# Retention, routed experts and a gated layer on one core: when weight conversions, piece remainders and routing steps are issued

## The chip, the cores and the metric

One core of a Trainium2 chip runs the whole program in one launch. The metric is the time of one launch in device microseconds (us); the profile's own span runs from the first to the last instruction of one profiled launch. TensorE (PE) multiplies, VectorE (DVE) and ScalarE (ACT) work on SBUF and PSUM, GpSimd (POOL) works on SBUF and issues the indirect DMAs, and the sync engine (SP) issues all other DMAs.

## The reference, cut to what matters

Three stages follow one another. Retention over 768 steps gives 3072 tokens of 512 numbers. The router gives each token to one of eight experts with room for 384 tokens each, in the order of the sorted logits; each expert is two matrix products with a relu. A gated layer then works on every token.

```python
# routed experts
order = np.argsort(-flat)                       # flat = (x @ w_gate).flatten()
for idx in order:                               # greedy, cap = N // E = 384
    tok, e = idx // E, idx % E
    if assigned[tok] >= 0 or counts[e] >= cap: continue
    assigned[tok] = e; counts[e] += 1
for e in range(E):
    out[mask] = np.maximum(x[mask] @ w1[e], 0.0) @ w2[e]
# gated layer
gate = 1.0 / (1.0 + np.exp(-(x @ w_gate)))
return gate * (x @ w_val) @ w_out
```

## The kernel before, in words

**Stages.** Retention runs first, 24 blocks of 128 tokens (lines 453 to 492), with 23 of 36 weight conversions woven in. The first routing phase follows alone (lines 822 to 823), then eight experts, each with its own 384 tokens: the expert's two products (h_step and y_step for eight column blocks f) and, for the same tokens, the gated layer (g_step and o_step for twelve column blocks g). While one expert is computed the routing of the next is found.

**Units.** One unit is twelve products of 128 x 384 (an h_step, a y_step, or the gate or value half of a g_step) or nine products of 128 x 512 (an o_step). After each unit hook() is called (lines 809 to 820): it runs the next piece of the next expert's routing if its delay has run out, and then whatever `late` holds for that unit number. An expert has 51 units, numbered from 0 in the first expert. PE, DVE, ACT and POOL each work in the order in which instructions are issued, so the place of a hook call in the code is its place in every queue.

**Routing.** members(x) (line 553) is a generator whose yields are delays in units. For the first expert it runs at once, on DVE with idle products that keep PE busy; for the later ones search4 (line 308) finds the cut in eight digits. Each digit has two halves: compare (cm, line 291), then, some units later, count on PE (line 299) with own, sm, ex on DVE (lines 301 to 304), then a small product on PE (line 318) with top, fl, ed, edb on DVE (lines 321 to 326) and the next compare. After the eighth digit come the positions, the comparison of line 643, the count of line 646 and the gather of the expert's tokens by three indirect DMAs on POOL (lines 532 to 535). turn_x transposes the gathered tokens in three turns; in the first expert the first turn comes at g == 8, in others at g == 7 (line 862).

**Pieces.** All products read weights split into a rounded part hi (ACT, line 664) and a remainder lo (DVE, line 665), made in a ring of six pieces in a fixed order (lines 679 to 723); ahead(key) makes pieces up to five beyond the one in use.

**Conversions.** The gated layer's weights come as 8-byte numbers; conv_steps (line 147) turns 512 columns into a float block of `wall`: ACT and DVE (lines 153, 154), DVE (156), ACT and POOL (158, 159), DVE (161). A conversion's last 13 of 36 run in the first expert, at units 7, 9, 12, ... by LATE: lines 154 and 156 at unit u, 158 and 159 at u + 1, 161 at u + 3.

Of the kernel before, what the change touches and what calls it, by code (L numbers as in the profile page):

```python
# [20 lines left out]
def retention_moe_glu_kernel(  # L21
# [285 lines left out]

    def search4(x):

        for n in range(8):  # L310
            cm = compare4()
            if n < 7:
                digit4(n + 1)
            yield 2
            ex = count4(cm)
            yield 2 if x == 1 else 1
            pd = psm.tile([128, 128], F32, name="pr")
            PE.matmul(pd, ones16, ex.rearrange("p t e -> p (t e)"), start=True, stop=True)
            if n < 7:
                top, fl, d = small("top", (128, 16)), small("fl4", (128, 16)), small("d", (128, 1))  # L320
                DVE.tensor_reduce(top, pd.rearrange("p (t e) -> p t e", e=E), AX, OP.max)
                DVE.tensor_scalar(fl, top, CAP - 0.5, None, op0=OP.is_gt, op1=OP.add, accum_out=d)
                ed = small("ed")
                DVE.scalar_tensor_tensor(ed, r["edb"], d, far_up, op0=OP.subtract, op1=OP.mult)
                r["edb"] = small("edb", dt=BF)
                DVE.scalar_tensor_tensor(r["edb"], r["d4"][:, n + 1, :], 1.0, ed, op0=OP.add, op1=OP.add)
            else:
                fl, f = small("fle", (128, 16, E)), small("f", (128, E))
                DVE.tensor_scalar(fl, pd.rearrange("p (t e) -> p t e", e=E), CAP - 0.5, None, op0=OP.is_gt)
                DVE.tensor_reduce(f, fl.rearrange("p t e -> p e t"), AX, OP.add)  # L330
                r["full"] = f
# [105 lines left out]

    EARLY = 23
    LATE = [7 + 5 * n // 2 for n in range(NP - EARLY)]
    RAWS = 3  # L440
    conv_at = {4 + n * 41 // EARLY: n for n in range(EARLY)}

# [60 lines left out]

    idxs, xT, W, XG = {}, {}, {}, {}
    def gather(dst, src, col):
        POOL.indirect_dma_start(out=dst, out_offset=None, in_=src,
                                in_offset=bass.IndirectOffsetOnAxis(ap=col, axis=0))
# [32 lines left out]
    def fetch_rest():  # L540

        rest = W[0][0][:, :, 512:]
        ACT.activation(rest[:, 0, :1], ident[:, :1], AF.Copy)
        src = w1[bass.ds(which[0], 1)].rearrange("o (a p) f -> p (o a) f", p=128)
        SP.dma_start(rest, src[:, :, 512:])
        for f in range(2, W2R):
            fetch_w2(0, f)
        for n in range(RAWS):
            conv_load(EARLY + n, main, RAWS)

    which = {}

    def members(x, begun=None):
# [10 lines left out]
        if x < E - 1:  # L564
# [7 lines left out]
            for n in range(NL if x == 0 else 0):  # L572
# [6 lines left out]
                if n + 1 < NL:  # L579
                    digit(n + 1)  # L580
                yield 3 if T > 64 else 2
                pr = psm.tile([128, 128], F32, name="pr")
# [20 lines left out]
            else:  # L603
                yield from search4(x)
                full = r["full"]
# [37 lines left out]
        cms = [compare(i, c0, c1, 128, smb, OP.is_equal) for i, (c0, c1) in enumerate(parts)]  # L643
        yield 3 if x == 1 else 4
        ps = psm.tile([128, 128], F32, name="pr")
# [7 lines left out]
        if x + 1 < E:  # L653
# [5 lines left out]
            DVE.tensor_scalar(r["pen"], w8, mx, -3.0e38, op0=OP.is_equal, op1=OP.mult)  # L659
            DVE.scalar_tensor_tensor(arow, arow, mx, arow, op0=OP.not_equal, op1=OP.mult)  # L660
        yield 1

# [35 lines left out]
    def make(n):  # L698
        while made[0] < min(n, len(order)):
# [11 lines left out]
            t = main.tile([128, 2, DT, 128], F32R, name="piece", bufs=RING)  # L711
            split(src, t[:, 0], t[:, 1], DVE)
            pieces[key] = t
# [18 lines left out]
    def h_step(x, f):  # L732
        w = use(("w1", x, f))
        p = psm.tile([128, CAP], F32, name="mm", bufs=3)
        for dt in range(DT):
            three(p, w, (xT[x][:, 0, dt, :], xT[x][:, 1, dt, :]), dt, dt == 0, dt == DT - 1)
        t = main.tile([128, 2, CAP], F32R, name="hT", bufs=2)
        ACT.activation(t[:, 0], p, AF.Relu)  # L738
# [4 lines left out]
    def y_step(x, f):  # L743
# [3 lines left out]
        for dt in range(DT):  # L747
            three(acc[0][dt], w, (hT[f][:, 0], hT[f][:, 1]), dt, f == 0, f == FB - 1)
        if f == FB - 1:
            t = main.tile([128, 2, DT, CAP], F32R, name="x2T")  # L750
            x2[0] = t
            for dt in range(DT):
                split(acc[0][dt], t[:, 0, dt, :], t[:, 1, dt, :])
        ahead(("w2", x, f))

    def g_step(x, g):
        t = x2[0]
        ps = []
        for kind in ("wg", "wv"):
            w = use((kind, x, g))  # L760
            p = psm.tile([128, CAP], F32, name="mm", bufs=3)
            for dt in range(DT):
                three(p, w, (t[:, 0, dt, :], t[:, 1, dt, :]), dt, dt == 0, dt == DT - 1)
            ps.append(p)
            hook()
            if kind == "wg":
                sg = main.tile([128, CAP], F32, name="sg", bufs=2)
                ACT.activation(sg, p, AF.Sigmoid)
        gv = main.tile([128, CAP], F32, name="gv", bufs=2)
        DVE.tensor_tensor(gv, ps[1], sg, OP.mult)  # L770
        gt = main.tile([128, 2, CAP], F32R, name="gT", bufs=2)
        split(gv, gt[:, 0], gt[:, 1])
        gT[g] = gt
        ahead(("wv", x, g))

    scat = []
    spacer = consts.tile([1, 1], F32, name="spacer")

    def o_step(x, g):
        w = use(("wo", x, g)).rearrange("p z a b -> p z (a b)")  # L780
        if g == 0:
            acc[1] = [psm.tile([128, M], F32, name="acc", bufs=4) for _ in range(NA)]
        for a in range(NA):
            r = slice(a * 128, (a + 1) * 128)
            p = acc[1][a]
            PE.matmul(p, gT[g][:, 0, r], w[:, 0], start=(g == 0), stop=False)  # L786
            PE.matmul(p, gT[g][:, 0, r], w[:, 1], start=False, stop=False)  # L787
            PE.matmul(p, gT[g][:, 1, r], w[:, 0], start=False, stop=(g == GB - 1))  # L788
        if g == GB - 1:
            for a in range(NA):  # L790
                o = main.tile([128, M], F32, name="o", bufs=3)
                if a % 2:
                    DVE.tensor_copy(o, acc[1][a])
                else:
                    ACT.activation(o, acc[1][a], AF.Copy)
                POOL.memset(spacer, 0.0)
                st = POOL.indirect_dma_start(
                    out=out, out_offset=bass.IndirectOffsetOnAxis(ap=idxs[x][:, a:a + 1], axis=0),
                    in_=o, in_offset=None)
                for s in scat:  # L800
                    tc.declare_no_dep(st.ins, s.ins, reason="rows of other tokens")
                scat.append(st)
        ahead(("wo", x, g))
# [28 lines left out]

    late = {}
    for n, u in enumerate(LATE):
        m = EARLY + n
        if n + RAWS < len(LATE):
# [5 lines left out]
    for x in range(E):  # L842
# [4 lines left out]
        for f in range(FB):  # L847
            if f + 1 < FB:
                h_step(x, f + 1)
                hook()  # L850
            y_step(x, f)
            hook()
        g_step(x, 0)
        turn = None
        for g in range(GB):
            if g + 1 < GB:
                g_step(x, g + 1)
            elif x + 1 < E:
                for _ in turn:
                    pass  # L860
                h_step(x + 1, 0)
            if g == (7 if x else 8) and x + 1 < E:
                assert job[0] is None
                turn = turn_x(x + 1)
            if turn is not None:
                next(turn, None)
            o_step(x, g)
            hook()

# [41 lines left out]
```

## Time and profile before

| what | us |
|---|---|
| median of three timed launches (lowest, highest) | 1124.16 (1123.57, 1124.96) |
| the profiled launch, its own time | 1123.29 |
| its span, first to last instruction | 1121.5 |
| retention | 0 to about 152 |
| first routing phase | about 152 to 184 |
| first expert, first product to the next expert's first product | 184.07 to 314.11 |
| a later expert | 115.3 |
| last expert's part with no routing left, and the stores | 1007 to 1121.5 |

In the page each engine has a busy share; in tables by window each row is one stretch with the busy time of each engine and the granted clock of PE; in a timeline each row is start, length, engine, line, operation, output and input, and in brackets the idle time before it with what ended it.

### The profile page before, as it was taken

Reading aid. Unit: us, or ns where it says so; the run is one execution under the profiler, and the core shown is the slowest. Engines: PE = TensorE matmul, PEld = TensorE weight load, DVE = VectorE, ACT = ScalarE, POOL = GpSimd, SP = SyncE. Lnnn points to the kernel's source line nnn. Section 1 sums busy time; section 2 is a strip of 40 time slices with the busy share of each in tenths; the row PEclk is TensorE's granted clock in tenths of the full one; section 3 lists DMA queues with packets and bytes.
Section 4 is the critical chain, followed back from the end, with each engine's and each line's share of the span. In section 5 each row is a group of like instructions: output and inputs, shape, how many; then the busy total and the mean of one; then the engine's idle time right before and its main releaser. Section 6 shows DMA issues by size and latency. Waiting matters only on the chain.

```text
span 1121.5 us, 18122 instructions
## 1 busy us (share of the span) xinstructions
PE 1088.5 (97%) x6964; PEld 1005.2 (90%) x6964; DVE 736.8 (66%) x1787; ACT 487.6 (43%) x955; POOL 134.9 (12%) x146
## 2 busy tenths in 40 slices
PE   8999999988799999999999999999999999999997
PEld 6988988977799999989998999999989999999996
DVE  4887876888667756775677666765676545554542
ACT  3666623554343444334434343344343434343442
POOL 4354401121110011001100110011001000100001
PEclk9999989999899999999999999999999999999999
DMA  9999916123320212012100310031103012101000
GB/s 218 282 261 292 247 39 217 57 75 87 120 76 1 101 31 75 1 57 76 66 11 10 122 57 20 1 132 47 30 1 132 17 60 79 54 23 54 1 1 29
DMA packets 109608, 91.42 MB, mean 82 GB/s; under 512 B 54737, under 2 KB 92625, under 8 KB 109521
## 3 DMA queue, kind: packets, MB, share of 16 engines
q1 hardware_dynamic: 105680, 77.67, 23.4%
q0 software_dynamic: 3840, 12.59, 3.4%
q8 instruction: 55, 0.90, 0.3%
q14 instruction: 33, 0.26, 0.1%
HBM read 77.66 MB, written 12.58 MB: 80 GB/s over the span
## 4 chain that ended last, share of the span: by engine, by line
PE 73%; issue 11%; DVE 11%; SPq 2%; ACT 1%; DMA 1%; POOL 1%; POOLq 0%; DVEq 0%; ACTq 0%
PE mm L726 13%; PE mm L728 12%; PE mm L727 12%; PE acc L786 5%; PE acc L788 5%; PE acc L787 5%; DVE piece L665 3%; PE acc L726 2%; PE acc L728 2%; PE acc L727 2%; PE pA L373 2%; PE pY L388 2%; PE pX L407 2%; PE pS L395 2%; PE pY L384 2%
## 5 line engine op out<-in xcount | busy, mean ns | idle before, releaser
L726 PE MATMUL mm<-x2T,piece 128*128 128x384 f32 x768 | 261.7, 341 | 0.4 <-ACT x2T L664 0.4
L728 PE MATMUL mm<-x2T,piece 128*128 128x384 f32 x768 | 258.4, 337 | 0.7 <-DVE x2T L665 0.7
L727 PE MATMUL mm<-x2T,piece 128*128 128x384 f32 x768 | 257.6, 335 | 0.0
L665 DVE TENSOR_TENSOR piece<-wall,piece 128x512 fp32r<-128x512 f32 x288 | 186.2, 689 | 0.0
L664 ACT ACTIVATE gT<-gv 128x384 fp32r<-128x384 f32 x96 | 50.5, 526 | 266.5 <-DVE gv L770 266.5
L664 ACT ACTIVATE piece<-wall 128x512 fp32r<-128x512 f32 x288 | 163.1, 617 | 0.0
L726 PEld LDWEIGHTS mm<-x2T,piece 128*128 128x128 f32 x768 | 144.5, 188 | 3.8 <-ACT x2T L664 0.7
L727 PEld LDWEIGHTS mm<-x2T,piece 128*128 128x128 f32 x768 | 144.4, 188 | 3.1
L728 PEld LDWEIGHTS mm<-x2T,piece 128*128 128x128 f32 x768 | 144.1, 188 | 1.0 <-DVE x2T L665 1.0
L770 DVE TENSOR_TENSOR gv<-mm,sg 128x384 f32<-128x384 f32 x96 | 53.1, 553 | 129.1 <-PE mm L728 127.9
L786 PE MATMUL acc<-piece,gT 128*128 128x512 f32 x288 | 117.5, 408 | 0.0
L788 PE MATMUL acc<-piece,gT 128*128 128x512 f32 x288 | 114.0, 396 | 0.0
L787 PE MATMUL acc<-piece,gT 128*128 128x512 f32 x288 | 113.4, 394 | 0.0
L738 ACT ACTIVATE hT<-mm 128x384 fp32r<-128x384 f32 x64 | 31.5, 492 | 151.7 <-PE mm L728 151.7
L739 DVE SCALAR_TENSOR_TENSOR hT<-mm,hT 128x384 fp32r<-128x384 f32 x64 | 35.7, 557 | 87.1 <-ACT hT L738 87.0
L665 DVE TENSOR_TENSOR gT<-gv,gT 128x384 fp32r<-128x384 f32 x96 | 54.3, 566 | 56.9 <-ACT gT L664 56.9
L726 PE MATMUL mm<-xT,piece 128*128 128x384 f32 x256 | 87.5, 342 | 1.0 <-ACT xT L664 1.0
L726 PE MATMUL acc<-hT,piece 128*128 128x384 f32 x256 | 86.9, 339 | 0.0
L728 PE MATMUL mm<-xT,piece 128*128 128x384 f32 x256 | 86.2, 337 | 0.4 <-DVE xT L665 0.3
L727 PE MATMUL mm<-xT,piece 128*128 128x384 f32 x256 | 85.8, 335 | 0.0
L728 PE MATMUL acc<-hT,piece 128*128 128x384 f32 x256 | 85.8, 335 | 0.0
L727 PE MATMUL acc<-hT,piece 128*128 128x384 f32 x256 | 85.6, 334 | 0.0
(163 smaller groups left out, 1780.2 us busy)
## 6 DMA issues: line engine op xcount, KB each, us to landing
w2s<-in_moe_w_dram SPq DMA_DIRECT2D x64, 256.0 KB, 2.7
w1s<-in_moe_w_dram SPq DMA_DIRECT2D x7, 2048.0 KB, 7.7
q<-in_q_dram SPq DMA_DIRECT2D x12, 512.0 KB, 5.9
k<-in_k_dram SPq DMA_DIRECT2D x24, 256.0 KB, 5.6
v<-in_v_dram SPq DMA_DIRECT2D x24, 256.0 KB, 5.7
raw<-in_moe_w_gate_dram SPq DMA_DIRECT2D x12, 512.0 KB, 5.3
raw<-in_moe_w_val_dram SPq DMA_DIRECT2D x12, 512.0 KB, 5.4
xd<-xs SPq DMA_DIRECT2D x24, 256.0 KB, 4.4
```

The source lines that it names most:

```text
L373: PE.matmul(ps[s][:, a, :], kT[i][r, a, :], q_of(i)[r, a, :], start=True, stop=True)
L664: ACT.activation(hi, src, AF.Copy)
L665: eng.tensor_tensor(lo, src, hi.bitcast(F32), OP.subtract)
L726: PE.matmul(p, w[:, 0, dt, :], r[0], start=start, stop=False)
L727: PE.matmul(p, w[:, 1, dt, :], r[0], start=False, stop=False)
L728: PE.matmul(p, w[:, 0, dt, :], r[1], start=False, stop=stop)
L738: ACT.activation(t[:, 0], p, AF.Relu)
L739: DVE.scalar_tensor_tensor(t[:, 1], p, 0.0, t[:, 0].bitcast(F32), op0=OP.max, op1=OP.subtract)
L770: DVE.tensor_tensor(gv, ps[1], sg, OP.mult)
L786: PE.matmul(p, gT[g][:, 0, r], w[:, 0], start=(g == 0), stop=False)
L787: PE.matmul(p, gT[g][:, 0, r], w[:, 1], start=False, stop=False)
L788: PE.matmul(p, gT[g][:, 1, r], w[:, 0], start=False, stop=(g == GB - 1))
```

## The change

Six edits.

1. Three of the 13 late conversions (numbers 23 to 25) are loaded at the end of retention and computed inside the first routing phase, by fill(0) at six places of members(0); their last DVE steps follow at units 0 and 1. Of the loads that stood in fetch_rest one is left there, two come at unit 3.
2. The remaining ten conversions run at units 7, 10, 13, ..., 34.
3. In the first expert the remainder of each output piece (kind "wo") is computed by POOL in place of DVE.
4. The hook of an h_step, a y_step and an o_step is called directly behind the unit's products, ahead of what DVE and ACT do with the result and of the next pieces; in a g_step the next pieces are now made ahead of the value half's hook.
5. The second expert's search has one unit between count and small product (before: two), the delay ahead of its gather is four units (before: three), and its first turn comes at g == 7.
6. In the last expert the last two o_steps are interleaved by row block, the last gT is made in three column chunks, and each store's copy is halved between ACT and DVE.

```diff
-            yield 2 if x == 1 else 1
+            yield 1
...
-    EARLY = 23
-    LATE = [7 + 5 * n // 2 for n in range(NP - EARLY)]
-    RAWS = 3
+    EARLY, RAWS = 23, 3
+    LATE = [7 + 3 * n for n in range(NP - EARLY - RAWS)]
...
+    for n in range(RAWS):
+        conv_load(EARLY + n, main, RAWS)
+
+    fills = [[], [(0, 1)], [(0, 2)], [(1, 1)], [(0, 1)], [(1, 2), (2, 3)]]
+
+    def fill(x):
+        if x == 0:
+            for n, k in fills.pop(0):
+                conv_step(EARLY + n, k)
...
-        for n in range(RAWS):
-            conv_load(EARLY + n, main, RAWS)
+        conv_load(EARLY + RAWS, main, RAWS)
...
                     digit(n + 1)
+                if n:
+                    fill(x)
                 yield 3 if T > 64 else 2
...
         cms = [compare(i, c0, c1, 128, smb, OP.is_equal) for i, (c0, c1) in enumerate(parts)]
-        yield 3 if x == 1 else 4
+        fill(x)
+        yield 4
...
             DVE.scalar_tensor_tensor(arow, arow, mx, arow, op0=OP.not_equal, op1=OP.mult)
+        fill(x)
         yield 1
...
-            split(src, t[:, 0], t[:, 1], DVE)
+            split(src, t[:, 0], t[:, 1], POOL if kind == "wo" and x == 0 else DVE)
...
             three(p, w, (xT[x][:, 0, dt, :], xT[x][:, 1, dt, :]), dt, dt == 0, dt == DT - 1)
+        if f:
+            hook()
         t = main.tile([128, 2, CAP], F32R, name="hT", bufs=2)
...
             three(acc[0][dt], w, (hT[f][:, 0], hT[f][:, 1]), dt, f == 0, f == FB - 1)
+        if f < FB - 1:
+            hook()
         if f == FB - 1:
...
                 split(acc[0][dt], t[:, 0, dt, :], t[:, 1, dt, :])
+            hook()
         ahead(("w2", x, f))
...
             ps.append(p)
+            if kind == "wv":
+                ahead(("wv", x, g))
             hook()
...
-        DVE.tensor_tensor(gv, ps[1], sg, OP.mult)
         gt = main.tile([128, 2, CAP], F32R, name="gT", bufs=2)
-        split(gv, gt[:, 0], gt[:, 1])
+
+        last = x == E - 1 and g == GB - 1
+        for c in ([slice(a * 128, (a + 1) * 128) for a in range(NA)] if last else [slice(0, CAP)]):
+            DVE.tensor_tensor(gv[:, c], ps[1][:, c], sg[:, c], OP.mult)
+            split(gv[:, c], gt[:, 0, c], gt[:, 1, c])
         gT[g] = gt
-        ahead(("wv", x, g))
...
+    def store(x, a):
+        o = main.tile([128, M], F32, name="o", bufs=3)
+        if x == E - 1:
+            ACT.activation(o[:, :256], acc[1][a][:, :256], AF.Copy)
+            DVE.tensor_copy(o[:, 256:], acc[1][a][:, 256:])
...
+    def last_blocks(x):
+        for g, a in ((GB - 2, 0), (GB - 2, 1), (GB - 1, 0), (GB - 2, 2), (GB - 1, 1), (GB - 1, 2)):
+            o_products(x, g, a)
+            if g == GB - 1:
+                store(x, a)
...
         for a in range(NA):
-            r = slice(a * 128, (a + 1) * 128)
...
+            o_products(x, g, a)
+        hook()
...
-    late = {}
+    late = {0: [(conv_step, EARLY + 1)], 1: [(conv_step, EARLY + 2)],
+            3: [(conv_load, EARLY + RAWS + 1, main, RAWS), (conv_load, EARLY + RAWS + 2, main, RAWS)]}
     for n, u in enumerate(LATE):
-        m = EARLY + n
+        m = EARLY + RAWS + n
...
-            if g == (7 if x else 8) and x + 1 < E:
+            if g == 7 and x + 1 < E:
...
+            if x == E - 1 and g >= GB - 2:
+                if g == GB - 1:
+                    last_blocks(x)
+                continue
             o_step(x, g)
-            hook()
```

## Rows read from the trace of the kernel before

**Rows 1.** Two stretches: us, busy time of each engine, PE clock, DMA share, GB/s

```profile
184.00:314.00 130.00, 115.92 (x649) 105.90 (x649) 102.93 (x245) 62.59 (x121) 21.86 (x17) 0.97 0.31 101
...
296.00:300.00 4.00, 4.00 (x12) 3.35 (x13) 1.29 (x2) 1.11 (x2) 0.41 (x2) 0.54 0.42 126
```

**Rows 2.** Waits of PE, first expert: us in total, times, longest

```profile
PE mm L673 <- DMA xg<-xd,idx: 6.1, 1, 6.1
PE pr L299 <- DVE cm L291: 4.0, 3, 1.5
PE pr L629 <- DVE sc L624: 1.4, 1, 1.4
PE pr L318 <- DVE ex L304: 1.1, 1, 1.1
...
PE mm L728 <- DVE x2T L665: 0.7, 1, 0.7
```

**Rows 3.** Waits of PE, from 316 us to the end

```profile
PE pr L318 <- DVE ex L304: 3.8, 10, 0.5
```

**Rows 4.** Timeline of PE around the second expert's first turn: start, length

```profile
289.49 0.34 PE L728 MATMUL mm<-x2T,piece 128*128 128x384 f32 x1
295.98 1.08 PE L673 MATMUL mm<-ident,xg 128*128 128x128 f32 x4 [6.15 <-DMA xg<-xd,idx]
...
300.25 0.34 PE L726 MATMUL mm<-x2T,piece 128*128 128x384 f32 x1
...
304.45 0.60 PE L673 MATMUL mm<-ident,xg 128*128 128x128 f32 x4
...
306.96 0.33 PE L726 MATMUL mm<-x2T,piece 128*128 128x384 f32 x1
```

**Rows 5.** Timeline of DVE in the first expert's gated layer

```profile
235.37 0.28 DVE L321 TENSOR_REDUCE top<-pr 128x16 f32<-128x128 f32 x1
...
236.75 0.42 DVE L154 TENSOR_SCALAR wall<-raw 128x512 int32<-128x512 int32 x1
...
237.82 0.69 DVE L161 SCALAR_TENSOR_TENSOR wall<-raw,wall 128x512 f32<-128x512 f32 x1
238.42 0.22 DVE L301 TENSOR_TENSOR own<-pr,same 128x64 f32<-128x64 f32 x1
...
239.74 0.54 DVE L770 TENSOR_TENSOR gv<-mm,sg 128x384 f32<-128x384 f32 x1
...
241.40 1.90 DVE L665 TENSOR_TENSOR piece<-wall,piece 128x512 fp32r<-128x512 f32 x3
```

**Rows 6.** Timeline of DVE in the third expert, a count's three instructions

```profile
455.26 0.22 DVE L301 TENSOR_TENSOR own<-pr,same 128x64 f32<-128x64 f32 x1
...
456.04 0.69 DVE L665 TENSOR_TENSOR piece<-w2s,piece 128x512 fp32r<-128x512 f32 x1
```

**Rows 7.** Timeline of DVE while POOL adds, first expert

```profile
211.41 1.46 DVE L665 TENSOR_TENSOR piece<-wall,piece 128x512 fp32r<-128x512 f32 x1
```

**Rows 8.** Timeline of POOL, same stretch

```profile
211.01 1.32 POOL L159 TENSOR_TENSOR wall<-wall,raw 128x512 int32<-128x512 int32 x1 [3.12 <-DVE wall L156]
```

**Rows 9.** Timeline of DVE in the first routing phase

```profile
165.00 0.16 DVE L587 TENSOR_SCALAR_CACHE_REDUCE fl<-pr 64x8 bf16<-64x8 f32 x1 [0.88 <-PE pr L284]
...
165.70 0.18 DVE L598 TENSOR_TENSOR edb<-ed,dig 128x24 bf16<-128x24 f32 x1
...
174.75 0.16 DVE L648 COPY sl<-pr 128x6 f32<-128x6 f32 x1 [0.75 <-PE pr L284]
```

**Rows 10.** Timeline of POOL, the first expert's gather

```profile
176.07 1.45 POOL L506 DMA_INDIRECT xg<-xd,idx  x1 [29.77 <-ACT piece L664]
177.83 0.95 POOL L506 DMA_INDIRECT xg<-xd,idx  x1 [0.30 <-issue]
```

**Rows 11.** Timeline of all engines at the end

```profile
1109.65 0.56 DVE L770 TENSOR_TENSOR gv<-mm,sg 128x384 f32<-128x384 f32 x1 [3.30 <-PE mm L728]
...
1113.22 0.96 POOL L797 DMA_INDIRECT out_dram<-o,idx  x1 [102.51 <-ACT o L795]
```

More of the change, by code (lines that the diff above doesn't have):

```diff
@@ L306, in count4, with search4 @@
         return ex
-    def search4(x):
+    def search4():
         for n in range(8):
@@ L603, in members @@
             else:
-                yield from search4(x)
+                yield from search4()
                 full = r["full"]
@@ L769, in g_step, with o_products @@
         gv = main.tile([128, CAP], F32, name="gv", bufs=2)
-        DVE.tensor_tensor(gv, ps[1], sg, OP.mult)
         gt = main.tile([128, 2, CAP], F32R, name="gT", bufs=2)
-        split(gv, gt[:, 0], gt[:, 1])
+        last = x == E - 1 and g == GB - 1
+        for c in ([slice(a * 128, (a + 1) * 128) for a in range(NA)] if last else [slice(0, CAP)]):
+            DVE.tensor_tensor(gv[:, c], ps[1][:, c], sg[:, c], OP.mult)
+            split(gv[:, c], gt[:, 0, c], gt[:, 1, c])
         gT[g] = gt
-        ahead(("wv", x, g))
     scat = []
     spacer = consts.tile([1, 1], F32, name="spacer")
+    def o_products(x, g, a):
+        w = use(("wo", x, g)).rearrange("p z a b -> p z (a b)")
+        r = slice(a * 128, (a + 1) * 128)
+        p = acc[1][a]
+        PE.matmul(p, gT[g][:, 0, r], w[:, 0], start=(g == 0), stop=False)
+        PE.matmul(p, gT[g][:, 0, r], w[:, 1], start=False, stop=False)
+        PE.matmul(p, gT[g][:, 1, r], w[:, 0], start=False, stop=(g == GB - 1))
+    def store(x, a):
[3 more added lines that the diff above has]
+            DVE.tensor_copy(o[:, 256:], acc[1][a][:, 256:])
+        elif a % 2:
+            DVE.tensor_copy(o, acc[1][a])
+        else:
+            ACT.activation(o, acc[1][a], AF.Copy)
+        POOL.memset(spacer, 0.0)
+        st = POOL.indirect_dma_start(
+            out=out, out_offset=bass.IndirectOffsetOnAxis(ap=idxs[x][:, a:a + 1], axis=0),
+            in_=o, in_offset=None)
+        for s in scat:
+            tc.declare_no_dep(st.ins, s.ins, reason="rows of other tokens")
+        scat.append(st)
+    def last_blocks(x):
[3 more added lines that the diff above has]
+                store(x, a)
     def o_step(x, g):
-        w = use(("wo", x, g)).rearrange("p z a b -> p z (a b)")
         if g == 0:
@@ L783, in o_step @@
         for a in range(NA):
-            r = slice(a * 128, (a + 1) * 128)
[L785 to L788, printed above, removed]
+            o_products(x, g, a)
+        hook()
         if g == GB - 1:
             for a in range(NA):
[L791 to L802, printed above, removed]
+                store(x, a)
         ahead(("wo", x, g))
@@ L849, in retention_moe_glu_kernel @@
                 h_step(x, f + 1)
-                hook()
             y_step(x, f)
-            hook()
         g_step(x, 0)
@@ L866, in retention_moe_glu_kernel @@
                 next(turn, None)
+            if x == E - 1 and g >= GB - 2:
+                if g == GB - 1:
+                    last_blocks(x)
+                continue
             o_step(x, g)
-            hook()
 _INS = ["q", "k", "v", "moe_w_gate", "moe_w1", "moe_w2", "moe2_w_gate", "moe2_w_val", "moe2_w_out"]
```

## Prediction, made before the changed kernel ran

> **What bounds the kernel now.** I read the table of windows first, to see which stretch loses time. In the first expert's 130 us PE is busy 115.9 and DVE 102.9 [rows 1]; a later expert takes 115.3 in all. So about 15 us are lost in one expert, and there DVE is the engine without room.
>
> The waits of PE in that stretch say how they are lost [rows 2]. One wait of 6.1 us is for the second expert's gathered tokens. Five waits of 4.0 + 1.4 + 1.1 = 6.5 us are for steps of the second expert's search on DVE, and 0.7 is for x2T: 7.2 on DVE together. In all the rest of the launch PE waits 3.8 us, ten times, always for ex of a count [rows 3]. Beyond these PE is the bound, and nothing in the change shortens its products: what can be won is these waits and what the clock does after them.
>
> **The gather's wait.** The last product ahead of it started at 289.49, the next gate product at 300.25 [rows 4]. The same first-turn work undisturbed (four transposes and the nine products of an output unit) goes from 304.45 to 306.96, 2.5 us. 300.25 - 289.49 is 10.8; 2.5 and one product's pace of 0.17 are natural; 8.1 us are lost, 2 of them because PE's granted clock was 0.54 in 296 to 300, that is near the lower of its two levels (1.2 against 2.4 GHz), after PE had done nothing for 6.15 us [rows 1, 4]. With one unit instead of two in each of eight digits the count ahead of the gather comes at unit 33 instead of 40; the first turn moves only from g == 8 to g == 7, so the gather stands some five units ahead of it, over 10 us, where there was one unit. Also on DVE sl and idx no longer stand behind gv, gT and three pieces. I take all 8.1 us as won.
>
> **The later experts.** There own, sm and ex follow hT and a piece, and PE wants ex one unit later. They take 456.04 - 455.26 = 0.8 us [rows 6], a unit 2.1 (half of the 4.2 from 300.25 to 304.45 [rows 4]). Called directly behind the products they are done in time. I take the 3.8 us [rows 3] as won. In g_steps two pieces now go first, 1.3 us; with 0.8 this is just inside the unit, so no new wait.
>
> **DVE in the first expert, the uncertain term.** With three units per digit I count one turn of three gated units. PE needs 6.3 (4.2 and 2.1), with the search's products about 6.6; with four transposes in their place it is 306.96 - 300.25 = 6.7 [rows 4]. DVE's work in a turn, start to start [rows 5, 6]: top to d 236.75 - 235.37 = 1.38 and the count 0.78; one conversion, 237.82 - 236.75 = 1.07 and 238.42 - 237.82 = 0.60; gv, the wait for ACT, and gT, 241.40 - 239.74 = 1.66; two pieces at 1.90 / 3, 1.27 (the third is POOL's). Sum 6.76. Before it was 0.75 digits, 1.2 conversions and three pieces: 1.62 + 2.00 + 1.66 + 1.90 = 7.2. The search coming faster eats most of what pieces and conversions give back.
>
> To this come the times in which POOL holds DVE up. The POOL addition from 211.01 lasts 1.32; the piece that DVE starts at 211.41 takes 1.46 [rows 7, 8], where three take 1.90: 0.8 more. In 238.42 to 239.74 the count takes 1.32 instead of 0.78: 0.5 more. The new remainder on POOL is of the same shape, with two inputs, so I price it like that addition: 1.3 on POOL, and on DVE between 0 and 1.3. Two POOL instructions per turn, each holding DVE 0.55 (nearest the 0.5 and 0.8 seen), make 6.76 + 1.1 = 7.9, 1.3 over PE's 6.6. Ends: 6.8 (none) and 9.4 (both in full).
>
> The Trainium skill, page "SBUF — State Buffer", section "Who interferes with whom", says that DVE with two SBUF inputs and GpSimd take one port pair as an exclusive lock, and the second to issue is fully blocked. The stretched piece agrees. By that rule taken whole the turn is the 9.4 end and the sum comes out as in the slow rival without its clock.
>
> Four gated turns lie between the first gate unit and the eighth digit (units 15 to 27): 4 x 1.3 = 5.2. In the h and y units three turns with conversions: 2.16 search, 1.67 conversion, three pieces 1.9, one and a half hT at gv's 0.54, 0.8, one hold 0.55: 7.1 against 6.6, 1.5 for three. x2T keeps its 0.7. The first 1.3 us of lag are free, since ex takes 0.8 of a unit's 2.1. New waits on DVE: 5.2 + 1.5 + 0.7 - 1.3 = 6.1, where 7.2 stood: 1.1 won. After unit 27 the search is over, so DVE may lag: pieces are made up to five ahead, and gT has three units.
>
> **The first routing phase.** Nine DVE steps of conversions go in. The first falls into a gap like the 0.88 and 0.75 us idle before fl and sl [rows 9]; so do the 0.7 us steps at the fourth digit and behind the last compare: nothing, while PE's count covers them, and 0.7 each without it. But the fourth digit's step frees a POOL addition of 1.32 at about 164.9, and edb, at 165.70, has two SBUF inputs: 0.5. Behind the gather's index DVE gets 0.7 + 0.4 + 0.7 more while POOL issues gathers; the first took 1.45 beside DVE's pieces, the second 0.95 [rows 10]: 0.5 for each of the other two, say 0.8 in all, on the path to the transposes. Two POOL additions queue behind the gathers and hold nobody. Sum +1.3, ends 0 and 2. The three loads stand on SP behind retention's last stores and ahead of the expert's weights, with some 15 us to spare; the two at unit 3 stand ahead of later w2 loads, whose ring is three deep. Two last steps of 0.6 at units 0 and 1 lie before the load on DVE begins.
>
> **The end.** gv starts at 1109.65 and the first store at 1113.22 [rows 11]. Interleaving has row block 0 ready 0.7 earlier, but the chunks go DVE, ACT, DVE three times ahead of DVE's half copy, so the first store starts about where it did: 0, ends -0.5 and +0.5.
>
> **Sum.** -8.1 - 1.1 - 3.8 + 1.3 = -11.7 on the profiled launch's 1123.3: 1111.6. The median of the runs stands 0.9 above the profiled launch: 1112.5.
>
> **Rivals.** *DVE freed.* POOL's work falls into DVE's reads of PSUM and its waits; a turn is 6.8 and new waits are 4 x 0.16 = 0.6, so 6.6 are won: -17.2, 1107. For it: gv, own and the reductions were not stretched; against: each conversion's addition is followed by pieces. Chance 0.16.
>
> *The lock.* The remainder comes just when DVE's next work is the gate piece with two SBUF inputs: 1.32 in full and 0.8 for the addition, a turn of 8.9. New waits 4 x 2.3 + 3 x 0.75 + 0.7 - 1.3 = 10.9: 3.7 lost, -8.1 + 3.7 - 3.8 + 1.3 = -6.9, 1117. For it: moved work costs twice as long on POOL. Chance 0.21. The same skill page's rule that issue order decides who blocks is this case.
>
> *The lock and the clock, slower.* Both POOL instructions hold in full, 4 x 2.8 + 3 x 1.3 + 0.7 - 1.3 = 14.5 of waits, which alone gives -8.1 + 7.3 - 3.8 + 1.3 = -3.3; and each turn's wait of 2.8 at a gated unit lowers the clock as the long one did (4.3 from 295.98 to 300.25 instead of 2.5, 1.8 each): +7.2, so +3.9, 1128. It decides where new waits and clock together pass 7.2 + 8.1 + 3.8 - 1.3 = 17.8. Against it: waits up to 1.5 us left no slow window but the one in 296 to 300. Chance 0.13, of which 0.04 end within the bound.
>
> *The gather is still waited for.* If DVE's lag delays idx by five units, 8.1 comes back: 1120.6, and with a little of the lock no change. It would make edit 5 fail at what it does. Chance 0.04.
>
> **How the numbers follow.** My forecast has 0.46. A measurement of this kernel tells about 0.2%, 2.2 us, from no change. Faster: 0.46 + 0.16 + 0.21 = 0.83; same: 0.04 + 0.04 = 0.08; slower: 0.09. The range goes from the freed case with routing at 0 and the end at -0.5 (1105) to the lock with routing at 2 and the holds in the h and y turns larger by 0.9 each (1120.5); it leaves out less than 0.2.
>
> **What would show it.** Right: no wait of PE on xg near the second expert's first turn and no clock near half there; no waits on ex after the second expert; waits on cm, ex or x2T of 4 to 8 us in units 7 to 27; the first expert near 120 us. POOL's 12 remainders at 1.2 to 1.4 each and DVE instructions stretched beside them. The first product of the first expert 0 to 2 us later than 184.07. Wrong: waits on DVE under 2 or over 10, a first product over 3 us later, or waits on hT or gT that were not there.

## The result and the profile after

The changed kernel takes 1110.82 us (median of 4 runs, 1109.77 to 1111.16) against 1124.32 us for the kernel before on the same chip: ratio 0.988, interval 0.986 to 0.990. It is faster by about 13.5 us; forecast were 1112.5, 11.7 saved. The profiled launch took 1110.73 us with a span of 1109.0.

PE's timeline shows where the time went when the launch is cut at each expert's first h product (its start is the first number of such a row). Lengths in us:

| stretch | before | after | difference |
|---|---|---|---|
| launch to the first h product | 184.07 | 185.33 | +1.3 |
| first expert | 130.04 | 122.51 | -7.5 |
| second expert | 116.01 | 114.25 | -1.8 |
| third to sixth expert, each | 115.34 | 114.25 | -1.1 (four: -4.4) |
| seventh expert | 111.52 | 111.53 | 0 |
| eighth expert and end | 118.54 | 118.36 | -0.2 |

The sum is -12.6, as between the spans of 1121.53 and 1108.97.

The same two stretches as in [rows 1], from the table of windows of the changed kernel:

```profile
184.00:314.00 130.00, 121.49 (x688) 110.95 (x687) 102.66 (x234) 63.17 (x121) 36.04 (x29) 1.00 0.28 94
296.00:300.00 4.00, 4.00 (x26) 3.88 (x25) 2.31 (x3) 1.85 (x4) 1.28 (x1) 1.00 0.00 0
```

PE is busy 5.6 us more and never below its full clock, and 296 to 300 is an ordinary stretch now. Two columns show the other side: DVE, which gave work to POOL, is as busy as before (102.7, before 102.9), and POOL's time rose by 14.

The waits of PE in the first expert answer to [rows 2]:

```profile
PE pr L318 <- DVE ex L304: 5.4, 5, 1.6
...
PE acc L804 <- ACT gT L676: 1.3, 1, 1.3
...
PE mm L740 <- DVE x2T L677: 0.8, 1, 0.8
```

The wait for the gathered rows is gone; cm and sc have gone too. In their place stand ex, five times, and one wait for gT that was not there. From 318 us to the end PE waits for nothing; [rows 3] had ten waits.

One turn of three gated units, on DVE, on POOL and on PE (start, length, engine, line):

```profile
237.74 0.69 DVE L677 TENSOR_TENSOR piece<-wall,piece 128x512 fp32r<-128x512 f32 x1
238.34 0.22 DVE L301 TENSOR_TENSOR own<-pr,same 128x64 f32<-128x64 f32 x1
238.59 0.27 DVE L303 TENSOR_REDUCE sm<-own 128x8 f32<-128x64 f32 x1
238.90 0.82 DVE L304 TENSOR_TENSOR ex<-spread,sm 128x128 f16<-128x128 f32 x1
239.97 1.45 DVE L677 TENSOR_TENSOR piece<-wall,piece 128x512 fp32r<-128x512 f32 x1 [0.25 <-ACT piece L676]
241.35 0.28 DVE L321 TENSOR_REDUCE top<-pr 128x16 f32<-128x128 f32 x1
...
246.09 0.68 DVE L677 TENSOR_TENSOR piece<-wall,piece 128x512 fp32r<-128x512 f32 x1
```

```profile
237.96 1.61 POOL L159 TENSOR_TENSOR wall<-wall,raw 128x512 int32<-128x512 int32 x1 [5.36 <-issue]
239.53 1.35 POOL L677 TENSOR_TENSOR piece<-wall,piece 128x512 fp32r<-128x512 f32 x1
```

```profile
239.78 0.23 PE L318 MATMUL pr<-ex,ones 128*128 128x128 f16 x1 [1.58 <-DVE ex L304]
...
248.13 0.23 PE L318 MATMUL pr<-ex,ones 128*128 128x128 f16 x1 [1.59 <-DVE ex L304]
...
256.37 0.23 PE L318 MATMUL pr<-ex,ones 128*128 128x128 f16 x1 [1.47 <-DVE ex L304]
```

The turn lasts 246.09 - 237.74 = 8.35 us on DVE, and PE's small product comes every 8.3 us, 1.5 late each time: DVE sets the pace. Two of its instructions are held. ex takes 0.82 while POOL adds (0.29 alone), the gate's piece 1.45 while POOL makes the output piece's remainder (0.68 alone). own, with an input in PSUM, and the reduction sm run beside the same addition at their usual 0.22 and 0.27.

### The profile page after: what moved, and what is told of

The parts are those of the page before. It is cut to its first block, busy times and chain, and to the rows that moved or that the text cites. A ratio compares the mean times of both kernels' runs of the same rounds, so it can differ in the third digit from the quotient of the medians.

```text
span 1109.0 us, 18222 instructions
## 1 busy us (share of the span) xinstructions
PE 1085.4 (98%) x6964; PEld 1004.3 (91%) x6964; DVE 742.4 (67%) x1781; ACT 490.1 (44%) x958; POOL 150.8 (14%) x158
## 4 chain that ended last, share of the span: by engine, by line
PE 79%; issue 10%; DVE 6%; SPq 1%; ACT 1%; DMA 1%; POOL 1%; POOLq 0%; ACTq 0%; DVEq 0%
PE mm L738 13%; PE mm L740 13%; PE mm L739 13%; PE acc L804 5%; PE acc L806 5%; PE acc L805 5%; PE acc L738 3%; PE acc L740 3%; PE acc L739 3%; PE pA L373 2%; PE pY L388 2%; PE pY L384 2%; PE pX L407 2%; PE pS L395 2%; PE pr L284 2%
## 5 line engine op out<-in xcount | busy, mean ns | idle before, releaser
L677 DVE TENSOR_TENSOR piece<-wall,piece 128x512 fp32r<-128x512 f32 x276 | 190.1, 713 | 106.6 <-ACT piece L676 104.3
L676 ACT ACTIVATE piece<-wall 128x512 fp32r<-128x512 f32 x288 | 169.3, 622 | 0.0
L676 ACT ACTIVATE gT<-gv 128x384 fp32r<-128x384 f32 (+1 forms) x98 | 50.8, 519 | 211.6 <-DVE gv L793 211.6
L787 ACT ACTIVATE sg<-mm 128x384 f32<-128x384 f32 x96 | 47.1, 490 | 136.9 <-PE mm L740 113.6
L677 DVE TENSOR_TENSOR gT<-gv,gT 128x384 fp32r<-128x384 f32 (+1 forms) x98 | 54.2, 554 | 62.3 <-ACT gT L676 62.3
L515 POOL DMA_INDIRECT xg<-xd,idx x24 | 24.7, 1030 | 445.5 <-issue 434.3
```

The source lines that it names most:

```text
L515: POOL.indirect_dma_start(out=dst, out_offset=None, in_=src, in_offset=bass.IndirectOffsetOnAxis(ap=col, axis=0))
L676: ACT.activation(hi, src, AF.Copy)
L677: eng.tensor_tensor(lo, src, hi.bitcast(F32), OP.subtract)
```

## The experiments

Unless another base is named, an edit is made to the changed kernel. "First expert" is the stretch of the table above: 122.51 in the changed kernel, 130.04 before.

### Part 3 alone undone, and part 3 doubled

```diff
-            split(src, t[:, 0], t[:, 1], POOL if kind == "wo" and x == 0 else DVE)
+            split(src, t[:, 0], t[:, 1], DVE)
```

> The changed kernel with one part undone: DVE computes the first expert's output-piece remainders again. In the changed kernel's trace a search turn between units 18 and 27 takes 8.3 us, in which the gate piece on DVE waits 0.25 for ACT and takes 1.45 instead of 0.68 beside POOL's remainder. Theory 'hold' (the remainder on POOL stops DVE for as long as it saves): the turn gains those 1.0 and pays 0.6 for the piece, so 7.9 to 8.0; PE's waits for ex 0.3 to 0.4 shorter per turn; all in all 0 to 2 us faster than the changed kernel (median 1109 to 1111). Rival 'relief' (POOL takes 0.6 per turn off DVE): the turn grows to 8.9, the first expert is 2 to 4 us longer, median 1113 to 1115.

Measured (e1): 1106.92 us (1106.41 to 1107.47), ratio 0.984 (0.982 to 0.986); first expert 119.32. It beats both kernels: the change's own third part costs 3.2 us of the first expert, more than the 0 to 2 I expected. The waits for ex fall by 0.5 in each of three turns, and the wait for gT by 1.15. A turn on DVE is 7.84 long, and ex alone is held in it:

```profile
237.27 0.69 DVE L677 TENSOR_TENSOR piece<-wall,piece 128x512 fp32r<-128x512 f32 x1
...
238.42 0.83 DVE L304 TENSOR_TENSOR ex<-spread,sm 128x128 f16<-128x128 f32 x1
...
245.11 0.68 DVE L677 TENSOR_TENSOR piece<-wall,piece 128x512 fp32r<-128x512 f32 x1
```

The other way round, the value pieces' remainders went to POOL too:

```diff
-            split(src, t[:, 0], t[:, 1], POOL if kind == "wo" and x == 0 else DVE)
+            split(src, t[:, 0], t[:, 1], POOL if kind in ("wo", "wv") and x == 0 else DVE)
```

> The changed kernel with the remainders of the wv pieces on GpSimd as well in the first expert. Theory of the hold (each remainder on GpSimd makes a DVE operation beside it wait, and takes more from DVE than it gives): the turn stays at 8.3 or grows to 8.9, with more of the DVE operations at their held lengths (piece 1.45 in place of 0.69), the first expert is 1 to 5 us longer than 122.5, median 1112 to 1116. Rival (relief: DVE is freed of 0.69 for each): the turn falls to 7.7, the first expert is about 3 us shorter, median 1107 to 1109.

Measured (e11): 1117.49 us (1116.66 to 1118.29), ratio 0.9935 (0.992 to 0.995); first expert 129.11, 6.6 longer. The hold theory has the direction, but both figures lie beyond its 5 us and its 1116. The groups of instructions say why. DVE's from 184 to 290 us, POOL's from 184 to 320 us (count | busy us, mean ns | idle before); first the kernel without remainders on POOL, then the changed one, then the one with two kinds of them:

```profile
L677 DVE TENSOR_TENSOR piece<-wall,piece 128x512 fp32r<-128x512 f32 x33 | 22.6, 712 | 2.2 <-ACT piece L676 2.1
L156 DVE SCALAR_TENSOR_TENSOR wall<-raw,wall 128x512 int32<-128x512 int32 x10 | 7.0, 698 | 0.3
```

```profile
L677 DVE TENSOR_TENSOR piece<-wall,piece 128x512 fp32r<-128x512 f32 x21 | 20.5, 979 | 4.5 <-ACT piece L676 4.5
L677 POOL TENSOR_TENSOR piece<-wall,piece 128x512 fp32r<-128x512 f32 x12 | 15.8, 1314 | 15.2 <-ACT piece L676 15.2
```

```profile
L156 DVE SCALAR_TENSOR_TENSOR wall<-raw,wall 128x512 int32<-128x512 int32 x10 | 13.4, 1337 | 0.3
L677 DVE TENSOR_TENSOR piece<-wall,piece 128x512 fp32r<-128x512 f32 x10 | 12.5, 1249 | 6.6 <-ACT piece L676 6.6
L677 POOL TENSOR_TENSOR piece<-wall,piece 128x512 fp32r<-128x512 f32 x24 | 33.5, 1398 | 38.5 <-ACT piece L676 38.4
```

Twelve pieces taken from DVE should have given it 12 x 0.71 = 8.5 us. They gave 22.6 - 20.5 = 2.1, and DVE idled 2.3 us more for ACT's half of a piece. With 23 pieces fewer, their time falls by 10.1, but the conversion's step L156 alone takes 6.4 more and ex 1.3 more (its eight take 5.6 us, there 4.3), and the idle time 4.4 more. In this kernel a turn grows to 9.1 us, and the clock joins in (windows of 2 us, and PE's timeline):

```profile
240.00:242.00 2.00, 1.40 (x5) 1.13 (x6) 1.37 (x2) 1.15 (x3) 1.68 (x2) 0.73 0.06 15
242.00:244.00 2.00, 2.00 (x7) 1.52 (x6) 1.86 (x9) 0.00 (x0) 0.00 (x0) 0.50 0.00 0
244.00:246.00 2.00, 2.00 (x12) 1.93 (x11) 1.35 (x3) 1.51 (x3) 0.00 (x0) 0.92 0.00 0
```

```profile
240.60 0.23 PE L318 MATMUL pr<-ex,ones 128*128 128x128 f16 x1 [2.17 <-DVE ex L304]
```

The granted clock fell to the lower of its two levels (0.50, 1.2 GHz) after PE had waited 2.17 us. The spell costs 2 x (0.27 + 0.50 + 0.08) = 1.7 us. A second one, 274 to 280, costs 1.7 again, 15 us behind the last wait of over 1 us.

Waits and clock together account for every first expert within 0.6 us, but for e3 (1.4). Waits are the recorded ones of PE behind the expert's first unit; the clock's cost is the sum over windows of 2 us of 2 x (1 - clock), windows in which PE waits throughout left out:

| kernel | first expert | waits | clock | waits and clock against the changed kernel | measured |
|---|---|---|---|---|---|
| changed | 122.51 | 7.5 | 0 | | |
| before | 130.04 | 13.7 | 1.8 | +8.0 | +7.5 |
| part 3 undone (e1) | 119.32 | 4.8 | 0 | -2.7 | -3.2 |
| part 3 doubled (e11) | 129.11 | 10.6 | 3.4 | +6.5 | +6.6 |
| conversions a unit earlier (e2) | 127.63 | 10.8 | 1.7 | +5.0 | +5.1 |
| old pace (e3) | 125.84 | 8.8 | 3.4 | +4.7 | +3.3 |
| old order (e4) | 129.04 | 11.0 | 3.4 | +6.9 | +6.5 |
| 13 conversions in the expert (e7) | 130.58 | 13.3 | 1.7 | +7.5 | +8.1 |
| new order on the kernel before (e8) | 132.37 | 15.6 | 2.3 | +10.4 | +9.9 |

### The order of the hooks (part 4): undone, and alone on the kernel before

```diff
 # h_step, y_step and o_step alike: the hook goes back behind the unit's evictions and pieces
-        if f:
-            hook()
         t = main.tile([128, 2, CAP], F32R, name="hT", bufs=2)
...
+        if f:
+            hook()
...
-            if kind == "wv":
-                ahead(("wv", x, g))
             hook()
...
+        ahead(("wv", x, g))
```

> The changed kernel with edit 4 undone: every hook behind what the unit's result and the next pieces need, as before. Theory 'ex was late behind hT and a piece': each later expert with a search takes 115.3 again instead of 114.25, that is 1.08 x 5 = 5.4 us, of which the profile's idle time shows 0.76 each; in the first expert the waits for ex grow too, by 0 to 3; in all 5 to 8.5 us slower, median 1116 to 1119. Rival 'the later experts gained from something else' (the pace or the conversions): they stay at 114.25 and only the first expert moves, median within 3 us of 1110.8.

Measured (e4): 1122.36 us (10 runs), ratio 0.998 (0.9966 to 0.9992); first expert 129.04, and the second to sixth 115.33 again. The waits of PE from 318 us on are back:

```profile
PE pr L318 <- DVE ex L304: 3.9, 10, 0.5
```

Without part 4 nearly all of the gain is gone: 5 x 1.08 = 5.4 in the later experts, as expected, and 6.5 in the first, where 0 to 3 were expected; ex is waited for 9.3 us there and the clock falls twice. The same edit alone, on the kernel before:

> The kernel before with edit 4 alone (hooks directly behind the products, pieces ahead of the value half's hook). Theory 'the order is worth what undoing it cost': later experts 114.25 for 115.33, 5.4 us; the first expert 5 to 7 us shorter, since sl and idx no longer stand behind gv, gT and three pieces and the gather is not waited for; median 1111 to 1114. Rival 'the first expert needs the lighter DVE and the pace': there the gather is still waited for by 4 us or more and only the later experts gain; median 1117 to 1120.

Measured (e8): 1122.62 us (10 runs), ratio 0.997 (0.996 to 0.999). Its waits of PE in the first expert:

```profile
PE mm L673 <- DMA xg<-xd,idx: 5.6, 1, 5.6
PE pr L299 <- DVE cm L291: 4.9, 3, 2.5
PE pr L318 <- DVE ex L304: 2.2, 3, 0.9
```

The later experts come to 114.25 by the order alone, but the gather is still waited for, cm more than before, and the first expert is 2.3 us longer than the old one. So the order alone gives the 6 us behind 316 us and loses part of it ahead: the rival's mechanism, though slower than its 1117 to 1120.

### The pace of the search (part 5) undone

```diff
-            yield 1
+            yield 2 if x == 1 else 1
...
-        yield 4
+        yield 3 if x == 1 else 4
...
-            if g == 7 and x + 1 < E:
+            if g == (7 if x else 8) and x + 1 < E:
```

> The changed kernel with edit 5 undone: two units between count and small product in the second expert's search, three ahead of its gather, first turn at g == 8. Theory 'the gather was won by the pace': PE waits again 4 to 7 us for the gathered tokens and runs at the lower clock behind it, while the waits for ex (5.4 us) fall below 3; together 3 to 7 us slower than the changed kernel, median 1114 to 1118. Rival 'DVE alone made the gather late': with a third fewer conversions and pieces on DVE the gather comes in time even at the old pace, the waits for ex go too, and the time is 2 to 5 us below the changed kernel's.

Measured (e3): 1114.34 us, ratio 0.990 (0.989 to 0.992); first expert 125.84. Slower, but not through the gather: PE does not wait for xg. Its first gather is issued at 292.08 and its first transpose runs at 295.59, just in time; in the changed kernel these are 277.30 and 285.47, with 8 us between. What is waited for instead:

```profile
PE pr L639 <- DVE sc L634: 2.7, 1, 2.7
PE pr L299 <- DVE cm L291: 2.5, 2, 2.3
PE pr L318 <- DVE ex L304: 2.4, 3, 1.5
```

The waits of 2.29 (at 248.75) and 2.72 (at 281.64) are each followed by a spell at the lower clock, 3.4 us lost in all. So the gather's wait goes by the new order with the lighter DVE (here), and by the new pace with the lighter DVE (e4); by the new order alone it stays (e8). The new pace alone was not run.

### The conversions (parts 1 and 2): undone, and moved

```diff
-    LATE = [7 + 3 * n for n in range(NP - EARLY - RAWS)]
+    LATE = [7 + 5 * n // 2 for n in range(NP - EARLY)]
...
-        if x == 0:
-            for n, k in fills.pop(0):
-                conv_step(EARLY + n, k)
+        pass
```

> The changed kernel with edits 1 and 2 undone: 13 conversions in the first expert from unit 7 on, at the old spacing of 2.5 units, none in the routing phase. Theory 'DVE is the bound in the turns': each conversion costs DVE 1.7 and a hold of 0.5; 1.2 instead of 1 per turn makes the turn 8.3 + 0.4 = 8.7, and three more lie in the stretch; the first expert is 2 to 4.5 us longer; the 0.6 us by which sl comes later in the routing phase goes: net 1.5 to 4 us slower than the changed kernel, median 1112.5 to 1115. Rival 'conversions were covered': the net is within 1 us.

Measured (e7): 1118.4 us, ratio 0.9936 (0.992 to 0.996); the first product comes at 184.06, the first expert takes 130.58. The loads and last steps of these conversions go back to their old places as well. Parts 1 and 2 together are worth 8.1 us in the expert, about twice the 2 to 4.5 I expected; what the wider spacing does in it was not separated from the three conversions moved. Six waits for ex then take 8.2 us, the clock 1.7.

```diff
-    LATE = [7 + 3 * n for n in range(NP - EARLY - RAWS)]
+    LATE = [6 + 3 * n for n in range(NP - EARLY - RAWS)]
```

> The changed kernel with the ten late conversions one unit earlier (6, 9, ... 33 for 7, 10, ... 34), so that in a gated turn their DVE steps stand right ahead of gv, which reads PSUM, and of DVE's wait for ACT, instead of ahead of a piece and a count. Theory 'hold by place': POOL's addition then runs beside gv and the wait; the 0.5 us that ex loses per turn goes, and ACT's step of line 158 no longer stands ahead of sg, so the POOL remainder starts 0.6 earlier: turn 7.3 to 7.8 instead of 8.3, the first expert 2 to 4 us shorter, median 1107 to 1109. Rival 'sum of work': only the work in a turn counts, not its place: the turn stays at 8.2 to 8.4 and the time within 1 us of the changed kernel's.

Measured (e2): 1115.58 us, ratio 0.9916 (0.990 to 0.993); first expert 127.63, longer where I expected it shorter, and by more than the rival's 1 us. The turn stays at 8.2 us (small products at 234.63, 242.82, 251.05, 259.20): moving the conversion by a unit only swaps which DVE instruction is held, here ex, at 1.20. The 5.1 us are lost ahead of and behind the turns: hT is waited for 1.4 at 220.66, ex 2.47 at 234.63, gT 1.28 at 283.69, and 284 to 288 runs at the lower clock.

With part 3 undone and the conversions wider apart:

```diff
-    LATE = [7 + 3 * n for n in range(NP - EARLY - RAWS)]
+    LATE = [4 + 4 * n for n in range(NP - EARLY - RAWS)]
...
-            split(src, t[:, 0], t[:, 1], POOL if kind == "wo" and x == 0 else DVE)
+            split(src, t[:, 0], t[:, 1], DVE)
```

> The run with output remainders on DVE (e1_wo_dve), and the ten late conversions every fourth unit from unit 4 (4, 8, ... 40) instead of every third from 7 to 34. Theory 'work per turn': between units 15 and 27 three conversions lie instead of four (0.75 instead of 1 per turn), so the turn of 7.8 falls to about 7.2 and the first expert from 119.3 to 116.5 to 118; median 1104 to 1106. Rival 'place counts': conversions no longer fall on the output units, where no search step stands, and the waits for ex or cm grow as much as the work falls; the first expert stays within 1 us of 119.3.

Measured (e9): 1107.86 us (1106.84 to 1111.18), ratio 0.985 (0.982 to 0.988); first expert 118.12, 1.2 less than without the spacing, just outside both what I expected (116.5 to 118, a median of 1104 to 1106) and the rival's 1 us. One turn of four has no conversion and takes 6.6 us, PE's own time; the others take 7.5 to 7.8. The medians of the two are not told apart; in its profile the first product came 0.6 later than in e1's (185.88, there 185.26).

### The first routing phase and the end

```diff
-    fills = [[], [(0, 1)], [(0, 2)], [(1, 1)], [(0, 1)], [(1, 2), (2, 3)]]
+    fills = [[], [(0, 1)], [(0, 2)], [(1, 1)], [(0, 1)], [(1, 1), (2, 2)]]
...
-    late = {0: [(conv_step, EARLY + 1)], 1: [(conv_step, EARLY + 2)],
+    late = {0: [(conv_step, EARLY + 1)], 1: [(conv_step, EARLY + 1), (conv_step, EARLY + 2)], 2: [(conv_step, EARLY + 2)],
```

> The changed kernel with one difference in the last fill: behind the gather's index DVE does the same three steps, but the two POOL additions and ACT's steps that stood there come at units 1 and 2 of the first expert. In the changed kernel the first gather's data counts as landed 5.4 us after its issue instead of 3.6, and the first product comes 1.26 us later than before, 0.45 of it lost at the fourth digit. Theory 'additions': two POOL additions directly behind the gathers (179.5 to 182.1) keep the first gather from being finished, so without them the transposes start 0.5 to 1.4 us earlier and the time falls by 0.8 (0.4 to 1.3) us. Rival 'DVE steps': DVE's conversion steps beside the gathers' issue keep POOL from writing them out; then the landing stays near 5 us and the start moves by less than 0.3.

Measured (e5): 1111.03 us, ratio 0.987 (0.9845 to 0.989), first expert 122.45. Inconclusive on the additions: POOL had nothing else in its queue, so that it still began them at 181.65, directly behind the third gather, though they were issued later. The profile shows another cause. The rows are there 3.7 to 3.8 us after each gather's issue, the first transposes start 5.2 after it, at 183.14, and until then PE runs its 40 idle products, at the lower clock (0.50 in 172 to 178). So, on the spaced kernel (e9), 28 of them in place of 40:

```diff
-    WA, WB, WC, WD, WE, WF, WG = 6, 1, 8, 12, 40, 6, 6
+    WA, WB, WC, WD, WE, WF, WG = 6, 1, 8, 12, 28, 6, 6
```

> The kernel of e9, with 28 idle products in place of 40 behind the index count of the first routing phase. Theory (the idle products, when they run at the lower clock, end after the first gathered rows are there and hold the first transposes back): the first unit's first h product comes 0 to 1.2 us earlier than e9's 185.88, the first expert stays at 118 to 119, median 1106 to 1108. Rival (the rows' landing alone sets the first transposes, and TensorE without work ahead of them starts the first expert at a lower clock): the start stays at 185 to 186, the granted clock of 184 to 200 falls below 1.00, and the first expert is 1 to 2 us longer, median 1108 to 1110.

Measured (e10): 1106.11 us (1105.12 to 1106.95), ratio 0.983 (0.981 to 0.985), first product at 184.69, first expert 118.53. PE's timeline of the kernel with 40, then with 28:

```profile
175.95 6.19 PE L175 MATMUL acc<-busy 128*128 128x256 bf16 x40
181.98 0.60 PE L685 MATMUL mm<-ident,xg 128*128 128x128 f32 x4
```

```profile
175.73 4.88 PE L175 MATMUL acc<-busy 128*128 128x256 bf16 x28
180.47 0.63 PE L685 MATMUL mm<-ident,xg 128*128 128x128 f32 x4
```

The transposes start as the idle products end, 5.2 and 3.9 us after the first gather's issue at 176.79 and 176.57. The first product comes 1.2 sooner, and the clock stays at 1.00 behind it. In this profile the theory is right; the medians of the two kernels are not told apart. It has the lowest median of all kernels run, below the changed one with intervals that do not touch.

```diff
-        last = x == E - 1 and g == GB - 1
+        last = False
...
-        if x == E - 1:
+        if False:
...
-            if x == E - 1 and g >= GB - 2:
+            if False:
```

> The changed kernel with edit 6 undone: the last two output units one after the other, gT in one piece, stores' copies whole. Theory (as predicted): the three chunks on DVE and ACT eat what the interleaving brings, and the stores are paced by POOL at 1.3 us each; the span is the same within 0.5 us. Rival: the end was shortened by a good part of the 0.7 us of a row block, and the time grows by 0.5 to 1.0 us.

Measured (e6): 1111.22 us, ratio 0.988 (0.986 to 0.990); the last stretch is 118.55 against 118.36. The new end is worth 0.2 us in the profile (118.36 to 118.38 in every kernel with it, 118.54 to 118.55 in the three without); in the medians it cannot be told.

## Why the prediction was right, step by step

The total came nearer than its terms: forecast were 11.7 us for the profiled launch, won were 12.6. The first expert gave 1.7 less than forecast and the later ones 2.3 more; that these errors nearly cancel is luck.

**The gather's 8.1: right.** No wait on xg, no lower clock in 296 to 300; the gather stands 8.2 us ahead of the first turn (277.30, 285.47), where over 10 were forecast. The cause was put too narrowly: with the old pace (e3) the wait is gone too, by the new order and the lighter DVE, and the pace is then worth 3.3 us in other waits.

**DVE in the first expert: mechanism right, size short.** Forecast were a turn of 7.9, 6.1 us of waits and a first expert 9.2 shorter; measured 8.35, 7.5 and 7.5. Of the 7.5, ex and x2T are 6.1, the sum that was forecast, but by luck: the forecast had four turns of 7.9, and there were three of 8.3 after a first one of 7.3 (224.11 to 231.43 on PE). The other 1.3 are a wait for gT (below). The step that was short in the turn is "each holding DVE 0.55": ex was held 0.53, the gate's piece 0.77, and ahead of it DVE waits 0.25 for ACT's half: 6.76 + 0.53 + 0.77 + 0.25 = 8.3. The work itself was counted well: with part 3 undone DVE's turn is 7.84 (237.27 to 245.11), which is 6.76, the third piece at 0.6 and one hold of 0.54. By the measured terms the remainder does not pay: 0.6 saved, 0.77 and 0.25 given; with the forecast 0.55 it just did.

The Trainium skill, page "SBUF — State Buffer", section "Who interferes with whom", makes the shared port pair an exclusive lock. The trace agrees: ex and the piece, both with two SBUF inputs, end 0.15 and 0.54 us behind the end of POOL's instruction, no more than a length of their own (0.29, 0.68), and own and sm are not stretched. POOL waits as well: its addition from 237.96, begun beside DVE's piece, takes 1.61, against 1.32 in [rows 8]. The turn of 9.4 that I drew from the rule did not come: ex started 0.94 and the piece 0.44 behind POOL's instruction, so neither was held for a whole one. With one more remainder per turn (e11) it came to 9.1. Small steps with one stream from SBUF were held as well: ed took 0.85 for 0.24 in the first routing phase, and in e11 si (128x24, one input) took 1.30 for 0.18, both beside a POOL instruction.

**"gT has three units": wrong, 1.3.** At 278.96 an output product waits for ACT's half of gT, a sign of being wrong that the prediction names. With the remainders on DVE (e1) this wait is 0.2. A part is the lag of the turns, carried on past unit 27: DVE starts P, the first step behind the search, 1.93 later than in e1, and PE is 1.5 later. Then two steps P, which the prediction put at nothing, are held by both POOL instructions:

```profile
263.90 2.54 DVE L644 SCALAR_TENSOR_TENSOR P<-sc,pr,AE 128x24 f32<-128x24 bf16 x2
```

```profile
263.51 1.65 POOL L159 TENSOR_TENSOR wall<-wall,raw 128x512 int32<-128x512 int32 x1 [6.05 <-PE mm L740]
265.11 1.29 POOL L677 TENSOR_TENSOR piece<-wall,piece 128x512 fp32r<-128x512 f32 x1
```

In e1, where POOL runs only the addition:

```profile
261.97 1.45 DVE L644 SCALAR_TENSOR_TENSOR P<-sc,pr,AE 128x24 f32<-128x24 bf16 x2
```

In the first routing phase, with POOL idle, they take 0.41. Behind P, DVE is 3.02 later than in e1, and 3.06 at the gv that this gT is made of. By these rows the hold of P by the remainder (1.1) is a larger part of the wait than the lag; no run separates the two.

**Later experts: forecast 3.8, measured 6.1.** The step "I take the 3.8 us [rows 3] as won" took the recorded wait for the loss. PE's timeline of the kernel before shows one such place:

```profile
455.53 0.34 PE L728 MATMUL acc<-hT,piece 128*128 128x384 f32 x1
456.18 0.23 PE L318 MATMUL pr<-ex,ones 128*128 128x128 f16 x1 [0.31 <-DVE ex L304]
```

Products start 0.17 apart, these two 0.65: 0.48 is lost where the row says 0.31, since a product's recorded 0.34 reaches past the start of the next. Ten waits lose 3.8 + 10 x 0.17 = 5.5, as measured by undoing part 4 (5.4). The second expert gave 0.7 more. Its first products waited for xT in the kernel before, of which the second, 0.65 behind its forerunner instead of 0.17, lies in this stretch:

```profile
314.39 0.34 PE L727 MATMUL mm<-xT,piece 128*128 128x384 f32 x1
315.04 0.45 PE L728 MATMUL mm<-xT,piece 128*128 128x384 f32 x1 [0.31 <-DVE xT L665]
```

I had read the waits of PE only behind 316 us. In the changed kernel the third turn's transposes, at 299.07, are long done, and the first products start 0.17 apart (307.84 and 308.01).

**Routing: forecast +1.3, measured +1.3, by other terms, which is luck.** These rows of the changed kernel answer to [rows 9, 10], on DVE, POOL and PE:

```profile
165.27 0.85 DVE L606 TENSOR_SCALAR ed<-edb,pr 128x24 f32<-128x24 bf16 x1 [0.25 <-PE pr L603]
...
175.20 0.16 DVE L659 COPY sl<-pr 128x6 f32<-128x6 f32 x1 [0.15 <-PE pr L284]
```

```profile
175.86 1.14 POOL L515 DMA_INDIRECT xg<-xd,idx  x1 [9.79 <-DVE free L667]
```

```profile
181.40 0.63 PE L685 MATMUL mm<-ident,xg 128*128 128x128 f32 x4 [1.85 <-POOL wall L159]
```

The hold of 0.5 that I put on edb falls on ed, 0.6 (0.85, before 0.24), and moves sl from 174.75 to 175.20. The 0.8 for the gathers did not come: the first is 1.14 long, not 1.45, and is issued 0.66 after sl, not 1.32. What made the 1.3 is the landing, in the view of the tile xg over this phase:

```profile
DMA to landing us min/median/max: 4.0/4.6/5.4
```

In the kernel before it is 3.4 to 3.8. Here the first rows were 5.4 us on their way, PE idled 1.85 ahead of the transposes, and the addition on POOL that the row names is only the last thing seen ahead of them. The conversions do not always bring this: e6, which has them all, lands in 3.5 to 4.0 and has its first product at 184.09, as early as the kernel before. But late landings were seen only with conversions there (changed kernel 5.4, e3 4.9, e2 4.6); in the kernel before, e7 and e8, without them, the latest are 3.8, 3.9 and 3.8. Why this launch landed late stays open. In the kernels with this routing phase unchanged the first product comes between 183.59 (e4) and 185.88 (e9), so the term lies between -0.5 and 1.8 by what the launch brings; the hold on ed hides in it.

**The end: 0, right within its range** (0.2 us won, e6).

**The rivals.** "DVE freed" and the gather still waited for did not come. "The lock" is half right: the hold is larger than forecast, less than in full. The clock of the slow rival did not come with waits of up to 1.6 us, but its mechanism is real and of the size I gave (1.8, measured 1.7 a spell): e11, e4 and e3 each show a spell behind a wait of 2.2 to 2.7, though not every spell has one (last section).

## What to carry to other kernels

Before moving work from DVE to GpSimd, look at what DVE does beside it: if that has two SBUF inputs, it pays with its own time, and so did two small steps with one. Here 2.1 of 8.5 us of DVE time were gained, and the first expert was 3.2 us longer. A short wait of PE costs more than its row says, so place steps that PE will want directly behind the products they read. And add up waits and granted clock by short windows for every variant: the two together, not the waits alone, told how long the first expert took in each variant.

## What was not expected of the hardware

Spells of the lower clock in the first expert were about 3.4 us long, 1.7 us lost, in five kernels (e2, e3, e4, e7, e11). But waits do not tell them in advance: 2.47 us at 234.63 in e2 was followed by none, 1.28 at 283.69 by one, and e4's second spell (274 to 280) comes 14 us behind the last wait of over 0.6, at 259.92. What decides was not settled.

The clock in the first routing phase is 0.50 to 0.64 in 160 to 172 in all profiles, and comes up at different times after it: 40 idle products took 4.53 us in the changed kernel and in the one before, 6.17 in e1 and 6.19 in e9. In e1 the first transposes start 5.2 us behind the gather's issue, in e6, where the idle products took 4.53, 4.1.
